# Attention with decay and a gated projection on one core: a fixed table of the order of work in place of a list scheduler

## The chip, the cores and the metric

The program runs on one core of a Trainium2 chip. The metric is the time on the device, in microseconds (us), from one launch; the kernel before took 556.66 us, the median of 3 runs (556.4 to 556.75). The core has five engines that follow their own instruction streams and wait for each other through semaphores: TensorE (PE in the profile, with its weight loads as PEld), VectorE (DVE), ScalarE (ACT), GpSimd (POOL), and SyncE (SP), which here issues the DMA transfers.

## The reference, cut to what matters

Eight batches of eight heads, 576 positions, head size 64. The output of the attention, with the heads side by side (512 columns), goes through a short causal convolution that makes a gate, a projection, the product, and a second projection.

```python
scores = scale * np.matmul(q, k.transpose(0, 1, 3, 2))
decay = cum[:, :, :, None] - cum[:, :, None, :]          # cum: running sum of log f
scores = np.where(causal, -1e9, scores + decay)
attn = np.exp(scores - np.max(scores, axis=-1, keepdims=True))
attn = attn / (np.sum(attn, axis=-1, keepdims=True) + 1e-09)
x = np.matmul(attn, v)                                    # per batch: 576 x 512
gate_pre = sum(conv_w[k] * xp[:, k:k + S, :] for k in range(5))
out = (sigmoid(gate_pre) * (x @ w_val)) @ w_out
```

## The kernel before, in words

The 64 heads are worked off as 32 pairs, four pairs to a batch. For a pair `i` the functions at L485 to L712 list its pieces of work:

- `load_pair`, `load_rest`: DMAs for q and k (`Xr`), v (`vt`) and, per head, a broadcast row of the decay (`dm`, `dl`); GpSimd masks the diagonal blocks (`sel`, L414).
- `plan_t` (from pair 4 on): `Xr` is split into a rounded part `Xh` (`TH`) and the rest `Xl` (`TL`, L494), so that three fast products replace a slow one.
- `plan_s`: scores on PE in three groups, `S` with u = 0 (blocks of 512 and 256 columns), u = 1 (384 and 128) and u = 2 (the last 64 rows, two banks). On each block DVE adds the decay and takes the row extreme (`red`, L562), ACT takes the exponential and its sum (`SX`, L566), DVE the reciprocal (`rec`), and `norm` scales the block (L375 on DVE and POOL, L373 on ACT).
- `plan_pt`: PE transposes the normalised blocks (`PT`, L607, L625, L626) into a bank, and ACT or DVE copies the bank out to `pt` (`PE`, L368).
- `plan_pv`: PE multiplies with v (`PV`, two halves), the result is copied out (`X`), split (`xh`, `xl`), and DVE makes five convolution taps (`conv`, L709; the first tap may stand on another engine, L375 or L373). For pairs 0 and 1 PE makes the taps (`CV`).
- `plan_moe`, per batch: the first projection (`Mv`, two pieces of six matmuls to a bank), the gating (`H`), a split (`hh`, `hl`, L755), the second projection (`Mo`), the copy out (`O`) and the store (`OD`).

Ahead of this stand the decay table, and the two weight matrices, decoded and split on DVE, ACT and POOL (`wv`, `wo`), in the first part of the run. Six groups of transposes of the identity (`warm`, L468) occupy PE while the first inputs are on their way.

A piece is a node of `Plan`: the engines that may run it with a cost for each, a function that emits its instructions, and what it reads and writes. `Plan.order` (L186) is a list scheduler: it keeps a clock per engine in a model, and takes again and again the piece that can start first, ties and near ties by a priority with tabled offsets (`OFF`, `PEN`, L47 to L88). In doing so it picks the engine of a piece that may run on several, and the PSUM banks that it takes (`seize`, `room`). Here is the choice itself:

```python
p, n, ts, t = min((p, n, ts, t) for ts, p, n, t in cand if ts <= t0 + SLACK[e])
if best is None or (ts, p) < best[:2]:
    best = (ts, p, n, e, t)
```

The instructions of each engine, and all DMAs together, are then bound to this order (L856 to L862), so an engine whose next instruction waits holds back all behind it. All eight PSUM banks are in use; a piece that takes a bank waits until its last user is done.

Of the kernel before, what the change touches and what calls it, by code (L numbers as in the profile page):

```python
# [37 lines left out]
BEGIN = {"PE": 0.7, "ACT": 2.0, "DVE": 0.7, "POOL": 0.6, "SP": 0.6, "DQ": 0.0}  # L38
LAG = {"PE": 0.17, "ACT": 0.2, "DVE": 0.17, "POOL": 0.25, "SP": 0.65, "DQ": 2.0, "bank": 0.15}
SAME = {"PE": 0.0, "ACT": 0.06, "DVE": 0.1, "POOL": 0.1, "SP": 0.0, "DQ": 0.0}  # L40
SLACK = {"PE": 0.0, "ACT": 0.0, "DVE": 0.0, "POOL": 0.0, "SP": 0.1, "DQ": 0.2}
SWITCH = 0.105
STICK = 319.71
PAIR = 0.002
PORT = {"rec", "TH", "TL", "norm", "conv", "hh", "hl", "xl", "xh", "sel", "wv", "wo", "cw", "start", "st0", "cut0", "cuth", "cutl"}
TICK, BUSY = 10.24 / 3, 3150.0
OFF = {  # L47
# [8 lines left out]
    "dec": (-55.39, -189.04, -128.16, 116.43, -6.04, -106.51), "diag": (-62.58, -70.54, 0.0, 0.0, 0.0, 0.0),  # L56
# [28 lines left out]
}  # L85
NONE = (0.0,) * 6


def phase(base):
# [5 lines left out]

# [808 lines left out]
```

## Time and profile before

| what | value |
|---|---|
| time, median of 3 runs | 556.66 us |
| the profiled execution: its span, first to last instruction | 555.8 us |
| PE busy | 524.2 us, 4412 matmuls |
| DVE busy | 455.7 us |
| ACT busy | 418.7 us |
| POOL busy | 280.2 us |
| mean granted clock of PE, as a share of full speed | 0.984 |

The time of the profiled execution by itself is its span; the median is 0.86 us above it. A busy share is a union over an engine's instructions, so a busy PE can still be in a pace slower than its best: the ends of matmuls are modelled. In lists of waits each row names the engine that waited, what it waited for, the total, the number and the longest. PEclk is the clock that PE was granted, 1.00 being 2.4 GHz and 0.50 being 1.2 GHz.

### The profile page before, as it was taken

The numbers are of one execution on the slowest core, as the hardware profiler recorded it, in microseconds if no ns is written. First come the engines' busy times: TensorE is split into PE (matmuls) and PEld (weight loads), VectorE is DVE, ScalarE is ACT, GpSimd is POOL, SyncE is SP. The second block draws the span as 40 slices with busy tenths as digits, with TensorE's granted clock in tenths as the row PEclk, the third lists the DMA queues.
The fourth block names the chain that finished last, engine by engine and source line by source line (L and its number), as shares of the span: only waits on it lengthen the run. The fifth ranks groups of instructions, "written<-read, shape, count | busy, mean of one in ns | idle before, by whom it ended". The sixth has DMA issues, their size and how long they took to land. (4 is left out here: it accounts for less than half of the span.)

```text
span 555.8 us, 12834 instructions
## 1 busy us (share of the span) xinstructions
PE 524.2 (94%) x4412; PEld 455.5 (82%) x4412; DVE 455.7 (82%) x1273; ACT 418.7 (75%) x1136; POOL 280.2 (50%) x377
## 2 busy tenths in 40 slices
PE   6687977999999999999999999999999999999997
PEld 5465765888889888898889978879888898989895
DVE  2987998988899988999788999889898887675560
ACT  2989888988867668678887978888998886673411
POOL 4223455576634823467456463645754688641200
PEclk8989897999999999999999999999999999999999
DMA  8867673545635575554565536855556544310102
GB/s 268 265 198 219 215 249 121 185 162 205 214 122 162 186 223 177 204 178 165 174 195 176 189 133 205 284 175 202 179 204 209 200 142 157 110 44 2 49 28 96
DMA packets 29905, 95.44 MB, mean 172 GB/s; under 512 B 3920, under 2 KB 3920, under 8 KB 29840
## 3 DMA queue, kind: packets, MB, share of 16 engines
q1 hardware_dynamic: 29696, 94.00, 51.1%
q8 instruction: 35, 0.57, 0.4%
q10 hardware_dynamic: 144, 0.62, 0.3%
q14 instruction: 30, 0.25, 0.2%
HBM read 84.69 MB, written 9.91 MB: 170 GB/s over the span
## 5 line engine op out<-in xcount | busy, mean ns | idle before, releaser
L566 ACT ACTIVATE P<-banks,negm 128x512 f32<-128x512 f32 (+3 forms) x256 | 132.0, 527 | 30.3 <-DVE negm L562 27.9
L562 DVE CUSTOM_DVE_ANT_0 banks<-banks,dm 128x512 f32<-128x512 f32 (+3 forms) x256 | 118.5, 517 | 20.2 <-PE banks L353 9.8
L709 DVE SCALAR_TENSOR_TENSOR gate<-x,cw,gate 128x576 f32<-128x576 f32 x120 | 106.3, 886 | 11.2 <-POOL gate L375 10.1
L353 PE MATMUL banks<-xh,wall 128*128 128x288 f32 x512 | 109.3, 299 | 0.6 <-DVE pt L368 0.3
L607 PE MATMUL banks<-ident,P 128*128 128x128 f32 x640 | 92.6, 283 | 15.2 <-ACT P L373 6.1
L353 PE MATMUL banks<-pt,vt 128*64 128x128 f32 (+2 forms) x1408 | 98.0, 293 | 0.2 <-ACT P L566 0.2
L607 PEld LDWEIGHTS banks<-ident,P 128*128 128x128 f32 x640 | 72.4, 142 | 29.6 <-ACT P L373 10.9
L353 PEld LDWEIGHTS banks<-pt,vt 128*64 128x64 f32 x1408 | 86.1, 138 | 11.9 <-issue 2.4
L414 POOL TENSOR_SCALAR_AFFINE_SELECT dm<-dm 128x256 f32<-128x256 f32 x126 | 60.1, 502 | 67.0 <-DMA dm<-decd 65.2
L353 PE MATMUL banks<-wall,hh 128*128 128x512 f32 x288 | 92.7, 403 | 0.4 <-ACT ot L782 0.4
L368 ACT COPY pt<-banks 128x512 f32<-128x512 f32 (+2 forms) x210 | 80.4, 448 | 11.3 <-PE banks L607 9.7
L353 PEld LDWEIGHTS banks<-xh,wall 128*128 128x128 f32 x512 | 83.7, 188 | 2.8 <-ACT P L566 0.9
L353 PE MATMUL banks<-xl,wall 128*128 128x288 f32 x256 | 75.4, 295 | 0.0
L373 ACT ACTIVATE P<-P,rz 128x256 f32<-128x256 f32 (+3 forms) x129 | 66.9, 571 | 3.4 <-DVE rz L576 3.2
L494 POOL TENSOR_TENSOR Xl<-Xr,Xh 128x640 fp32r<-128x640 f32 (+1 forms) x40 | 61.8, 1548 | 7.8 <-ACT Xh L368 6.1
L353 PE MATMUL banks<-Xh 128*128 128x288 f32 (+4 forms) x280 | 58.4, 343 | 3.6 <-DVE pt L368 1.6
L353 PEld LDWEIGHTS banks<-wall,hh 128*128 128x128 f32 x288 | 50.8, 188 | 9.7 <-ACT ot L782 0.7
L353 PE MATMUL banks<-wall,hl 128*128 128x512 f32 x144 | 56.5, 393 | 0.0
L368 DVE COPY pt<-banks 128x256 f32<-128x256 f32 (+2 forms) x110 | 46.0, 450 | 12.8 <-PE banks L607 6.2
L353 PE MATMUL banks<-Xh,Xl 128*128 128x288 f32 (+4 forms) x280 | 53.1, 313 | 0.0
L353 PE MATMUL banks<-Xl,Xh 128*128 128x288 f32 (+4 forms) x280 | 52.9, 313 | 0.0
L566 ACT ACTIVATION_READ_ACCUMULATOR P<-banks,negm 128x1 f32 x256 | 52.1, 204 | 0.0
(108 smaller groups left out, 873.7 us busy)
## 6 DMA issues: line engine op xcount, KB each, us to landing
dm<-decd SPq DMA_DIRECT2D x62, 640.0 KB, 5.2
Xr<-in_x_dram SPq DMA_DIRECT2D x31, 608.0 KB, 4.3
vt<-in_v_dram SPq DMA_DIRECT2D x32, 320.0 KB, 5.2
out_dram<-ot SPq DMA_DIRECT2D x36, 256.0 KB, 2.5
dl<-decd SPq DMA_DIRECT2D x62, 144.0 KB, 4.4
wu<-in_w_val_dram SPq DMA_DIRECT2D x2, 512.0 KB, 4.9
ot<-in_w_val_dram SPq DMA_DIRECT2D x2, 512.0 KB, 5.5
ot<-in_w_out_dram SPq DMA_DIRECT2D x2, 512.0 KB, 4.6
```

The source lines that it names most:

```text
L353: nc.tensor.matmul(out, lhsT=lhsT, rhs=rhs, start=start, stop=stop)
L368: (eng.copy if eng is nc.scalar else eng.tensor_copy)(out=out, in_=in_)
L373: eng.activation(out=out, in_=in_, func=AF.Copy, scale=col)
L414: nc.gpsimd.affine_select(out=t, in_=t, pattern=[[0, 2], [-1, P]], base=0, channel_multiplier=1, compare_op=ALU.is_ge, fill=-BIG)
L494: eng.tensor_tensor(out=Xl[r][:, a:e], in0=Xr[r][:, a:e], in1=Xh[r][:, a:e].bitcast(F32), op=ALU.subtract)
L562: nc.vector.tensor_tensor_reduce(out=sl, in0=sl, in1=add[:, o:o + ext], op0=ALU.add, op1=ALU.min, scale=-0.125, scalar=3.0e38, accum_out=n ...
L566: nc.scalar.activation(out=dst[:, o:o + ext], in_=bank(key)[:, c0:c0 + ext], func=AF.Exp, bias=negm[r][:, col], scale=-1.0, accum_out=zs[r ...
L607: nc.tensor.transpose(out=bank(key)[:, c:c + P], in_=Pt[m][:, BOFF[b] + P * j:BOFF[b] + P * j + P], identity=ident)
L709: eng.scalar_tensor_tensor(out=gt, in0=src, scalar=wt_, in1=gt, op0=ALU.mult, op1=ALU.add)
```

## The change

`Plan.order` no longer decides anything. A string of digits in base 64 (`TABLE`) holds, for each of the 2868 pieces that issue something, its number, its engine, and the banks that it takes; `order` reads it from front to back, and the functions are called in that order. The clocks, priorities, penalties and bank lists of the scheduler are gone, and with them a rule by which a piece that took a bank had to wait, in the list, for whatever the bank's later users depend on (`loose`). Some costs in the calls are other numbers (`S`, `PV`, `PT`, `SD`, `TH`, `rec`, `cut0`); nothing reads them any more. The pieces, their instructions and the buffers are the same.

```diff
@@ class Plan
-    def order(self, begin):
...
-            for e in ready:
-                cand = []
-                for n in ready[e]:
-                    nd = nodes[n]
-                    t = max(clock[e], at[n][e])
...
-            _, _, n, e, t = best
-            nd = nodes[n]
-            for x in nd["engs"]:
-                ready[x].remove(n)
-            for k in sorted(nd["take"], key=lambda k: -self.width[k]):
-                self.home[k] = self.seize(self.width[k], t)
...
-            self.trace.append((t, end, e, n))
+    def order(self, table):
+
+        at, done = 0, {nd["ends"]: n for n, nd in enumerate(self.nodes) if nd["ends"] is not None}
+        seen = set()
+        while at < len(table):
+            n, e = DIGITS.index(table[at]) * 64 + DIGITS.index(table[at + 1]), ENGINES[int(table[at + 2])]
+            nd = self.nodes[n]
+            at += 3
+            assert nd["deps"] <= seen and e in nd["engs"]
+            for k in nd["take"]:
+                self.home[k] = range(int(table[at]), int(table[at]) + self.width[k])
+                at += 1
+            seen.update((n, done.get(n, n)))
             yield nd["fn"], e
+        assert len(seen) == len(self.nodes)
...
-        for k in touch:
-            t = self.taker[k]
-            if t != n and k not in self.loose:
-                self.nodes[t]["deps"].update(d for d in deps if d < t)
...
-            pe("PV", (1.36, 1.47)[half], p, go, [*vk, *(("pt", m, n) for m in ms for n in names), *(("pt0", m) for m in ms)], [key],
+            pe("PV", (1.36, 1.515)[half], p, go, [*vk, *(("pt", m, n) for m in ms for n in names), *(("pt0", m) for m in ms)], [key],
...
-    for fn, e in plan.order(BEGIN):
-        if fn is not None:
-            fn(e)
+    for fn, e in plan.order("".join(TABLE.split())):
+        fn(e)
```

The table's first line of digits, for its form:

```
0240630040B30930C40E10b20430u000r010N40s000a20c20d10520F20H20I10G20z30e20J20f23k40q010h10K20g20740Y40L20k10l12940i20j20M20P10m42b30Q20S20T10R20U20V20v
```

The order of the pieces is another on every engine. Three places follow. In the rows below, line numbers of the changed kernel are about a hundred lower, since it is shorter: L507 there is L607 before, L253 is L353, L275 is L375, L314 is L414. A trailing `x4` counts equal instructions in a row.

**PE, the first transposes.** This is PE's stream in the kernel before, from the first transposes of pair 0 (`P0`, `P1` are its heads, `Pl0` its last rows) over scores of pair 1 (`Xr1`) to the second part of pair 0's transposes.

```order
L607 MATMUL banks_125<-ident_64,P0_79 128x128 x4
L607 MATMUL banks_125<-ident_64,P1_80 128x128 x4
L607 MATMUL banks_125<-ident_64,P0_79 128x128 x2
L607 MATMUL banks_125<-ident_64,P1_80 128x128 x2
L353 MATMUL banks_125<-Xr1_74 128x512 x2
L353 MATMUL banks_125<-Xr1_74 128x256 x2
L353 MATMUL banks_125<-Xr1_74 128x288 x2
L607 MATMUL banks_125<-ident_64,P0_79 128x128 x4
L607 MATMUL banks_125<-ident_64,P1_80 128x128 x4
L625 MATMUL banks_125<-ident_64,Pl0_82 128x128 x4
L626 MATMUL banks_125<-ident_64,Pl0_82 64x128
```

And the same place in the changed kernel:

```order
L368 MATMUL banks_125<-ident_64 128x128 x4
L507 MATMUL banks_125<-ident_64,P1_80 128x128 x2
L507 MATMUL banks_125<-ident_64,P0_79 128x128 x4
L507 MATMUL banks_125<-ident_64,P1_80 128x128 x4
L507 MATMUL banks_125<-ident_64,P0_79 128x128 x2
L253 MATMUL banks_125<-Xr1_74 128x384 x2
L253 MATMUL banks_125<-Xr1_74 128x128 x2
L253 MATMUL banks_125<-Xr1_74 128x512 x2
L253 MATMUL banks_125<-Xr1_74 128x256 x2
L253 MATMUL banks_125<-Xr1_74 128x288 x2
L507 MATMUL banks_125<-ident_64,P0_79 128x128 x4
L507 MATMUL banks_125<-ident_64,P1_80 128x128 x4
```

One of the six groups on the identity now stands in front of the first transposes, the blocks are transposed in another order, and the scores of pair 1 with 384 and 128 columns, which stood behind pair 0's transposes, stand in front of the second part of them.

**PE, the fifth pair.** In the kernel before, this follows the first half of pair 3's product with v: the scores of pair 4 with 512 and 256 columns (`Xh0`, `Xl0`), then at once the first transposes of pair 4 (`P2`), then the other half of pair 3's product (`pt0`, `vt1`).

```order
L353 MATMUL banks_125<-Xh0_75 128x512 x2
L353 MATMUL banks_125<-Xh0_75,Xl0_77 128x512 x2
L353 MATMUL banks_125<-Xl0_77,Xh0_75 128x512 x2
L353 MATMUL banks_125<-Xh0_75 128x256 x2
L353 MATMUL banks_125<-Xh0_75,Xl0_77 128x256 x2
L353 MATMUL banks_125<-Xl0_77,Xh0_75 128x256 x2
L607 MATMUL banks_125<-ident_64,P2_81 128x128 x4
L353 MATMUL banks_125<-pt0_84,vt1_88 64x192
```

In the changed kernel those scores stand further up, between transposes of pair 3, and the next transposes of pair 4 come behind these rows, a half of the product with v (12 rows like `banks_125<-pt0_84,vt1_88 64x128`), and five transposes of `Pl0`:

```order
L253 MATMUL banks_125<-xh0_97,wall_122 128x288
L253 MATMUL banks_125<-xl0_103,wall_122 128x288
L253 MATMUL banks_125<-xh0_97,wall_122 128x288
L253 MATMUL banks_125<-xh1_98,wall_122 128x288
L253 MATMUL banks_125<-xl1_104,wall_122 128x288
L253 MATMUL banks_125<-xh1_98,wall_122 128x288
L253 MATMUL banks_125<-Xh1_76 128x384 x2
L253 MATMUL banks_125<-Xh1_76,Xl1_78 128x384 x2
L253 MATMUL banks_125<-Xl1_78,Xh1_76 128x384 x2
L253 MATMUL banks_125<-Xh1_76 128x128 x2
L253 MATMUL banks_125<-Xh1_76,Xl1_78 128x128 x2
L253 MATMUL banks_125<-Xl1_78,Xh1_76 128x128 x2
```

A first half of a projection of batch 0, which needs only pairs 0 and 1 (`xh0`, `xl0`, `xh1`, `xl1`), and the scores of pair 5 (`Xh1`) with 384 and 128 columns have moved in front of pair 4's transposes. On the whole, counted over all pairs, PE changes between transposes or projections, scores, and products with v 131 times instead of 144.

**POOL, the first 30 us.** GpSimd's stream in the kernel before, from where the setup ends; `u32` and `h32` are the convolution's diagonal weights, `dm` and `dl` decay rows, `wall` the decoded weights, and `P<-P,rz` a normalisation.

```order
L690 TENSOR_TENSOR u32_111<-ident_64,cw_66 128x512
L375 TENSOR_SCALAR h32_112<-ident_64,cw_66 128x128
L441 MEMSET dm1_69 128x1280
L414 AFFINE_SELECT dm1_69<-dm1_69 128x2x128 x2
L442 MEMSET dl0_71 128x576
L417 TENSOR_TENSOR dl0_71<-dl0_71,tri_65 128x64
L414 AFFINE_SELECT dm2_70<-dm2_70 128x2x128 x2
L414 AFFINE_SELECT dm0_68<-dm0_68 128x2x128 x2
L417 TENSOR_TENSOR dl1_72<-dl1_72,tri_65 128x64
L375 TENSOR_SCALAR P0_79<-P0_79,rz0_93 128x128
L414 AFFINE_SELECT dm1_69<-dm1_69 128x2x128 x2
L417 TENSOR_TENSOR dl0_71<-dl0_71,tri_65 128x64
```

The same stretch in the changed kernel:

```order
L374 MEMSET tri_65 128x64
L376 AFFINE_SELECT tri_65<-tri_65 64x64 x2
L317 TENSOR_TENSOR dl0_71<-dl0_71,tri_65 128x64
L275 TENSOR_SCALAR P0_79<-P0_79,rz0_93 128x512
L275 TENSOR_SCALAR P1_80<-P1_80,rz0_93 128x512
L314 AFFINE_SELECT dm2_70<-dm2_70 128x2x128 x2
L275 TENSOR_SCALAR P0_79<-P0_79,rz0_93 128x384
L380 MEMSET x320_95 128x4
L314 AFFINE_SELECT dm0_68<-dm0_68 128x2x128 x2
L275 TENSOR_SCALAR Pl0_82<-Pl0_82,rz0_93 128x576
L590 TENSOR_TENSOR u32_111<-ident_64,cw_66 128x512
L275 TENSOR_SCALAR h32_112<-ident_64,cw_66 128x128
```

The clearing of `dm1` and `dl0` has gone to DVE, and four normalisations of pair 0 stand here where one stood, with the diagonal weights behind them.

Over the whole run the pieces that may run on more than one engine are shared out as follows:

| piece | DVE before, now | ACT before, now | POOL before, now |
|---|---|---|---|
| `norm` | 91, 75 | 143, 137 | 54, 76 |
| `PE` (copies of transposes) | 110, 103 | 210, 217 | |
| `X` (copies of the product with v) | 45, 18 | 19, 46 | |
| `conv` (the first tap) | 4, 2 | 2, 17 | 24, 11 |
| `TH` | 0, 14 | 25, 24 | 31, 18 |
| `TL` | 16, 29 | | 40, 27 |
| `hl` | 13, 21 | | 19, 11 |
| `xh` | 2, 9 | 30, 23 | |
| `xl` | 17, 14 | | 15, 18 |
| `O` | 8, 13 | 28, 23 | |
| `hh` | 6, 10 | 26, 22 | |
| `sel` (the small addition) | 2, 12 | | 30, 20 |

The load of the first pair's q and k, on ACT's queue before, is SP's sixth issue now.

## Rows read from the trace of the kernel before

**Rows 1.** The page: busy time of each engine with its share of the span, and the granted clock in 40 equal slices, in tenths.

```profile
PE 524.2 (94%) x4412; PEld 455.5 (82%) x4412; DVE 455.7 (82%) x1273; ACT 418.7 (75%) x1136; POOL 280.2 (50%) x377
...
PEclk8989897999999999999999999999999999999999
```

**Rows 2.** Busy time of each engine in stretches of the run (us from the span's start; number of instructions in brackets), then granted clock, DMA share and GB/s.

```profile
0.00:9.60 9.60, 5.05 (x26) 4.84 (x26) 3.60 (x12) 3.04 (x6) 2.96 (x19) 0.99 0.82 281
9.60:120.00 110.40, 92.63 (x698) 72.04 (x698) 96.44 (x275) 93.88 (x248) 52.77 (x70) 0.92 0.64 209
60.00:80.00 20.00, 18.33 (x142) 14.10 (x142) 18.49 (x44) 17.59 (x44) 11.76 (x15) 0.99 0.70 240
120.00:540.00 420.00, 414.49 (x3638) 368.95 (x3639) 355.56 (x988) 318.77 (x879) 224.44 (x289) 1.00 0.49 163
540.00:555.80 15.80, 12.04 (x54) 9.63 (x52) 0.10 (x1) 2.99 (x5) 0.00 (x0) 0.99 0.23 84
```

**Rows 3.** What PE waited for from 0 to 120 us: total us, times, longest us. There are twelve such rows, 21.9 us in all.

```profile
PE banks L607 <- ACT P L373: 5.8, 7, 2.0
PE banks L353 <- DVE gate L821: 3.1, 1, 3.1
PE banks L607 <- ACT P L566: 2.6, 1, 2.6
PE banks L607 <- POOL P L375: 2.0, 1, 2.0
...
PE banks L468 <- POOL ebias L431: 1.4, 1, 1.4
PE banks L353 <- DVE pt L368: 1.1, 2, 0.9
...
PE banks L625 <- ACT Pl L373: 0.2, 1, 0.2
```

**Rows 4.** The same from 120 us to the end: nine rows, 5.0 us in all; the first, the second, and the last.

```profile
PE banks L607 <- DVE x L368: 1.7, 2, 1.4
PE banks L353 <- DVE pt L368: 0.8, 2, 0.5
...
PE banks L353 <- ACT P L566: 0.2, 1, 0.2
```

**Rows 5.** The sum over the three stretches between 12.8 and 540 us in which the granted clock is 0.50: 29.86 to 33.27, 57.16 to 60.58 and 84.47 to 91.30 us. Columns as in rows 2.

```profile
sum 13.66, PE 12.37 PEld 9.14 DVE 11.65 ACT 11.55 POOL 4.26; mean PE 4.12 PEld 3.05 DVE 3.88 ACT 3.85 POOL 1.42
```

**Rows 6.** PE's timeline: start, duration, instruction and count, and in brackets the idle time before it with what ended it.

```profile
25.17 1.24 PE L353 MATMUL banks<-Xr 128*128 128x288 f32 x4 [1.41 <-ACT Pl L566]
28.99 1.19 PE L607 MATMUL banks<-ident,P 128*128 128x128 f32 x8 [2.58 <-ACT P L566]
...
55.82 0.63 PE L607 MATMUL banks<-ident,P 128*128 128x128 f32 x4 [1.95 <-POOL P L375]
```

**Rows 7.** PE's timeline from 78 to 86 us, in the same form.

```profile
78.21 0.29 PE L353 MATMUL banks<-Xl,Xh 128*128 128x288 f32 x1
78.43 0.45 PE L353 MATMUL banks<-Xh 64*128 64x384 f32 x2
...
79.45 1.75 PE L353 MATMUL banks<-pt,vt 128*64 128x128 f32 x24
81.54 0.50 PE L353 MATMUL banks<-Xh 64*128 64x512 f32 x2 [0.34 <-ACT Pl L566]
...
83.79 0.39 PE L353 MATMUL banks<-Xh 64*128 64x256 f32 x2 [1.29 <-ACT P L566]
...
85.57 1.27 PE L607 MATMUL banks<-ident,P 128*128 128x128 f32 x4 [1.15 <-ACT P L373]
```

**Rows 8.** The chain that ended last, in order of time: start, duration, engine, line and count.

```profile
405.24 0.44 PE banks L607 x4
...
419.56 0.80 PE banks L353 x6
```

**Rows 9.** Groups of instructions over the whole run: count, busy us and mean ns of one, then the engine's idle time before them.

```profile
L494 POOL TENSOR_TENSOR Xl<-Xr,Xh 128x640 fp32r<-128x640 f32 (+1 forms) x40 | 61.8, 1548 | 7.8 <-ACT Xh L368 6.1
...
L375 POOL TENSOR_SCALAR P<-P,rz 128x512 f32<-128x512 f32 (+3 forms) x48 | 32.8, 694 | 35.2 <-DVE rz L576 25.4 <-ACT wall L368 2.8 <-ACT gate L798 2.4
...
L368 DVE COPY x<-banks 128x192 f32<-128x192 f32 (+1 forms) x45 | 19.6, 447 | 8.1 <-PE banks L353 7.9
...
L494 DVE TENSOR_TENSOR Xl<-Xr,Xh 128x576 fp32r<-128x576 f32 (+1 forms) x16 | 14.1, 895 | 0.0
...
L368 ACT COPY x<-banks 128x384 f32<-128x384 f32 (+1 forms) x19 | 7.6, 405 | 11.1 <-PE banks L353 10.9
```

**Rows 10.** The timeline of all engines at the start: the load of the first pair, and PE's first weights from it.

```profile
0.83 0.38 ACTq L380 DMA_DIRECT2D Xr<-in_x_dram  x1
...
11.85 0.80 PEld L353 LDWEIGHTS banks<-Xr 64*128 64x128 f32 x4
```

**Rows 11.** The convolution taps on DVE from 440 to 480 us.

```profile
L709 DVE SCALAR_TENSOR_TENSOR gate<-x,cw,gate 128x576 f32<-128x576 f32 x12 | 10.3, 854 | 0.1
```

**Rows 12.** The same taps from 500 to 540 us.

```profile
L709 DVE SCALAR_TENSOR_TENSOR gate<-x,cw,gate 128x576 f32<-128x576 f32 x12 | 12.5, 1043 | 8.3 <-POOL gate L375 8.0
```

**Rows 13.** The engines in these two stretches, columns as in rows 2.

```profile
440.00:480.00 40.00, 40.00 (x344) 36.08 (x342) 32.38 (x96) 29.10 (x86) 33.95 (x46) 1.00 0.37 127
500.00:540.00 40.00, 40.00 (x308) 36.72 (x307) 24.45 (x44) 11.73 (x26) 5.45 (x7) 1.00 0.07 27
```

More of the change, by code (lines that the diff above doesn't have):

```diff
@@ L37 @@
 MS = 0.2222
[L38 to L45, printed above, removed]
@@ L86 @@
-NONE = (0.0,) * 6
-def phase(base):
-    return sum(base >= x for x in (0.95, 3, 6, 11, 28))
+ENGINES = ("PE", "ACT", "DVE", "POOL", "SP")
+DIGITS = "0123456789abcdefghijklmnopqrstuvwxyzABCDEFGHIJKLMNOPQRSTUVWXYZ-_"
+TABLE = """
+0240630040B30930C40E10b20430u000r010N40s000a20c20d10520F20H20I10G20z30e20J20f23k40q010h10K20g20740Y40L20k10l12940i20j20M20P10m42b30Q20S20T10R20U20V20v
+002d001232e02l20W10y32j22o0452m12h23a40X30o40_22x062f20A32k12i12r22t20w30-
+12c32g12s10t001122n23c42B31212E11742Q002p22q12v22w13e44n42K012u12y24t43g44r42z12C32D23i41021323m32M022N12O032P22R21422L12A24l41512G12I11621i43z0453p02
@@ L94, with __init__ @@
+03LL3LR2LO2LS2LT2M40LZ2LW2L-2L_2Md01M22M52M62M72M800M90GB2Ma1GC4Me0Mf1Mb4Mi00Mj0Mk1Mg4Ml4Mn01Ms00Mo0Mp1Mt0Mq4Mu1Mv4
+"""
 class Plan:
-    def __init__(self, banks):
+    def __init__(self):
         self.nodes = []
-        self.free = {n: 0.0 for n in range(banks)}
         self.home = {}
@@ L113, in __init__, with bank @@
         self.width = {}
-        self.users = {}
-        self.taker = {}
-        self.loose = set()
-    def bank(self, key, width=1, loose=False):
+        self.taken = set()
+    def bank(self, key, width=1):
         self.width[key] = width
-        if loose:
-            self.loose.add(key)
         return key
@@ L136, in add @@
             self.readers[k] = []
-        take, touch = [], []
-        for k in (*writes, *reads):
-            if k in self.width and k not in touch:
-                touch.append(k)
-                self.users.setdefault(k, []).append(n)
-                if k not in self.taker:
-                    self.taker[k] = n
-                    take.append(k)
-        deps.discard(n)
-        self.nodes.append(dict(cls=cls, engs=engs, base=float(prio), phase=phase(prio), prio=prio * PAIR + OFF.get(cls, NONE)[phase(prio)], fn=fn, deps=deps, take=take, touch=touch,
-                               cols=cols, mode=mode, ends=ends))
-        for k in touch:
-            t = self.taker[k]
-            if t != n and k not in self.loose:
-                self.nodes[t]["deps"].update(d for d in deps if d < t)
+        touch = list(dict.fromkeys(k for k in (*writes, *reads) if k in self.width))
+        take = [k for k in touch if k not in self.taken]
+        self.taken.update(take)
+        deps.discard(n)
+        self.nodes.append(dict(cls=cls, engs=engs, base=float(prio), fn=fn, deps=deps, take=take, touch=touch, cols=cols, mode=mode, ends=ends))
         return n
@@ L160, in dma @@
         return m
-    def seize(self, width, t):
-        fit = [n for n in self.free if all(self.free.get(n + k, 1e18) <= t + 1e-9 for k in range(width))]
-        n = min(fit) if width == 1 else max(fit)
-        for k in range(width):
-            del self.free[n + k]
-        return [n + k for k in range(width)]
-    def room(self, widths):
-        for t in sorted(set(self.free.values())):
-            at = sorted(n for n in self.free if self.free[n] <= t)
-            left = list(at)
-            for w in sorted(widths, reverse=True):
-                fit = [n for n in left if all(n + k in left for k in range(w))]
-                if not fit:
-                    break
-                n = min(fit) if w == 1 else max(fit)
-                for k in range(w):
-                    left.remove(n + k)
-            else:
-                return t
-        return None
@@ L514, in plan_s @@
                 name = ("S", i, h, u, j if u == 0 else 0)
-                keys[n] = new(name, 2 if u == 2 else 1, loose=i == 0)
+                keys[n] = new(name, 2 if u == 2 else 1)
             pairs = ((0, 1), (2, 3))
@@ L724, in plan_moe @@
             for half, (lo, hi) in enumerate(((0, 288), (288, 576))):
-                key = new(("Mv", b, jj, half), loose=b == B - 1 and jj < 2)
+                key = new(("Mv", b, jj, half))
                 p = m0 + MS * (2 * jj + half)
```

180 lines of the change are left out of this document (76 added, 104 removed), and 17 rows, old and new, of tables (OFF, PEN).

## The prediction

> **What bounds the kernel now.** I read the page first [rows 1]: PE is busy 94% of the span, DVE 82%, ACT 75%, POOL 50%. The reader is to see that the granted clock is below full in the first fifth of the slices alone. Then the engines by stretch [rows 2]: from 120 to 540 us PE is busy 414.5 of 420 us, while from 9.6 to 120 us it is busy 92.6 of 110.4 us and DVE and ACT 96.4 and 93.9. So there are two regimes: a long one in which PE sets the pace and the others run beside it, and a first one in which PE, DVE and ACT take turns in waiting. Then PE's waits [rows 3, 4]: 21.9 us of the listed ones lie before 120 us, 5.0 us after it. Of the early ones 4.5 us belong to the start (1.4 and 3.1, for the identity and the decay table); 17.4 us are waits for normalised blocks, for banks and for copies. Then the clock: three stretches of 0.50 [rows 5] hold 13.66 us, with PE busy in 12.37 of them. At full speed that work would take half, so up to 6.2 us are lost there. The two waits from 25 to 29 us [rows 6] come just ahead of the first of these, the wait of 1.95 ahead of 55.82 just before the second, the three near 82 to 86 us [rows 7] around the third.
>
> The Trainium skill says on its front page ("Trainium Kernel Development and Optimization", "Performance Expectations") that matmul busy time is a poor measure of how near a kernel is to its limit. Here the trace agrees: the stretches at half clock count as 12.37 us busy [rows 5]. By the page's rule the 94% is no floor; by the row alone the gain could not pass the span less the busy time, 31.6 us. The sum below stays far under that.
>
> **The change part by part.** No instruction is added or removed, so nothing is paid for in kind. The pace of the tail is fixed: from 540 us on PE runs only the last projection [rows 2], which needs everything before it; I cost it at nothing. What the order does I take in five terms.
>
> *1. Waits from 9.6 to 120 us.* At pair 4, in the kernel before, PE has from the end of the 384 and 128 column scores (79.45) to the first transposes only a half of a product with v (1.75) and one scores group (79.45 - 78.43 = 1.02) to do, 2.8 us; the blocks were ready 6.1 us after the scores, at 85.57, and 0.34 + 1.29 + 1.15 us of waiting stand between [rows 7]. In the new order I count behind the same scores 15 transposes at 0.11 (0.44 for four), half a projection at 0.80 [rows 8], two scores groups at 1.02 and two halves of products at 1.75 [rows 7]: 1.65 + 0.80 + 2.04 + 3.5 = 8.0 us, more than 6.1. These waits should go. At pair 0 the scores of pair 1 that moved up cover about 1 us of the 3.99 us waited there [rows 6], and four normalisations stand on POOL where one stood, which spares ACT. Over the whole program I counted, at the fastest tenth of each kind's start-to-start times in the trace, the PE work between a scores group and each of its 224 transposing pieces: it is under 5 us for 20 of them before and for 3 now, under 8 us for 70 before and for 23 now.
>
> How much of it becomes time is set by what else is full. The work that DVE and ACT have to do up to the same point of PE's stream is about the same (pieces counted along both orders, with the trace's durations, give 1% more on DVE and 2% more on ACT by the time PE has done 80 us of work at its best pace). DVE is busy 96.4 of 110.4 us there. The fullest stretch that the rows show is 18.49 of 20 us, 92.5% [rows 2]. At that share 96.4 us of work take 104.3 us: 6.1 us less than now. The waits and the clock together offer 17.4 + 6.2 = 23.6 us, so DVE is what limits it. The bounds are 0 (the waits move, DVE's share stays at 87%) and 14 us (DVE without a gap); I take 6.1, by the row. At the very start nothing is expected: PE waits there for the decay table, which hangs on the load of f. The two clearings that go to DVE lie in its idle time (3.60 of 9.60 us busy [rows 2]); if that cover were gone they would delay the table by their length.
>
> *2. Waits after 120 us.* Of 5.0 us [rows 4] I take off 3, about the share by which short distances to the scores become rarer (70 to 23); bounds 0 and 5.
>
> *3. Turns of PE between kinds of work*, 144 to 131. At 78.21 the last full-width matmul is followed by scores 0.22 us later, where six such matmuls take 0.80, 0.13 each [rows 7, 8]: 0.09 a turn, 13 x 0.09 = 1.2 us less. Bounds: nothing, and twice as much.
>
> *4. Copies of transposes.* Of the 64 halves of products with v, 17 have under 4 us of PE work between their last transposes and themselves before, 32 now. PE waited for such a copy four times, 1.9 us in all, at most 0.9 [rows 3, 4]. Over the 17 close ones that is 0.11 each, so 15 more cost 1.7 us. Bounds: nothing, and 15 x 0.9 = 13.5 us, each as late as the worst.
>
> *5. Work that changes engine.* DVE gets 13 of the subtractions `TL` at 0.895, but gives 27 copies `X` at 0.447 away to ACT, where one takes 0.405 [rows 9]; with all lines of the table of the change I make it some 11 us more on DVE, 11 more on ACT and 40 less on POOL. From 120 us on DVE is busy 85% and ACT 76% [rows 2]; 11 us more in 420 is under 3 points each, so PE's work hides it: cost 0. The bound above is all 11 us, if DVE were on the path throughout; below, 0. The load of the first pair's q and k moves from ACT's queue to behind five issues on SP. PE took its first weights from it at 11.85, 11 us after the issue [rows 10], so a few microseconds of delay are hidden; past that each would delay the first scores.
>
> The Trainium skill speaks against the mix in "SBUF — State Buffer", section "Who interferes with whom": a DVE instruction with two SBUF inputs and a GpSimd instruction that reads SBUF exclude each other. The taps are of that kind, and the trace has them at 854 ns where POOL is busy 33.95 of 40 us, and at 1043 ns where it is busy 5.45 [rows 11 to 13]: the trace does not show POOL slowing them. By the rows the term is 0; by the rule see the last rival.
>
> Sum against the execution's own time: 555.8 - 6.1 - 3.0 - 1.2 + 1.7 = 547.2; the median of the runs stood 0.86 above that span, so 548.1 us.
>
> **Rivals.** *More goes than DVE's fullest stretch suggests.* If DVE runs without a gap up to 120 us: -14, -5, -1.2 and no cost in copies: 535.6 + 0.9 = 536.5. For it: POOL is busy 52.8 of 110.4 us, so more of DVE's share could be taken over. Against: DVE gets more work, not less.
>
> *The waits only move.* DVE's share stays at 87% up to 120 us and the late waits come back as waits for banks: -1.2 + 1.7, so 557.2. For it: at 81.54 and 83.79 PE waited for banks, not for blocks [rows 7], and the new order holds more scores in the same eight banks at once. Against: the counted distances.
>
> *Copies late (slower).* The halves of products with v stand nearer to their transposes, and the copies between them sit in the queues of DVE and ACT, each with 11 us more to do. At 0.9 us for each of 15 [term 4]: 555.8 - 6.1 - 3.0 - 1.2 + 13.5 = 559.0, 559.9 as a median. It decides from about 0.7 us each, where 15 of them eat the 10.3 us of gains. Against: in the trace these waits are short.
>
> *DVE and POOL in each other's way (slower).* 22 more normalisations on POOL at 0.694 [rows 9] are 15.3 us; if each held a DVE instruction back for its length and DVE were on the path: 548.1 + 15.3 = 563.4. This is the rule of the SBUF page, against which [rows 11 to 13] stand, and POOL has 40 us less to do in all.
>
> **How the numbers follow.** Forecast 0.63, with its own range of 541 to 554 us (early waits from 0 to 12 us); more goes, 0.09; waits only move, 0.10; copies late, 0.12; DVE against POOL, 0.04; between the forecast's range and no change, 0.02. What a measurement can tell from no change is 0.2%, 1.1 us, so 555.5 to 557.8 counts as the same. Faster is 0.63 + 0.09 + 0.02 = 0.74, same 0.10, slower 0.16. The likeliest case gives 548.1. A range of 540 to 559 leaves out most of the first rival below and the worse half of the slower ones above, some 0.18 together.
>
> **What would show it.** Term 1 is right if from 9.6 to 120 us the listed waits of PE fall well below 17 us, the stretches of half clock near 30, 57 and 85 us get fewer or shorter, and DVE's share rises over 90%; the stretch around pair 4's transposes should show no wait of a microsecond. It is wrong if PE's waits there carry other names (banks, `X`) with the same total. Term 4 is wrong if PE's waits for `pt` exceed 5 us. Term 5 is wrong if DVE's share from 120 us on rises over 92% and PE's busy share there falls. The forecast fails as a whole if PE, from 120 us on, is idle more than 10 us.

## The result, and the profile after

The changed kernel takes 540.42 us, the median of 4 runs (539.51 to 541.72), against 556.7 us for the kernel before on the same chip: a ratio of 0.9702, 95% interval 0.9666 to 0.9738, 16.3 us less. The forecast was 548.1 us. The time lies in the range of 540 to 559, but at its lower edge, and 0.6 us outside the range that the likeliest case had for itself (541 to 554). The profiled execution has a span of 539.0 us, 16.8 less than before.

The page of the kernel after, the lines of [rows 1]:

```profile
PE 515.9 (96%) x4412; PEld 448.6 (83%) x4412; DVE 468.1 (87%) x1288; ACT 424.5 (79%) x1160; POOL 241.9 (45%) x338
...
PEclk9999999999999999999999999999999999999999
```

The same 4412 matmuls count as 8.3 us less of busy PE, and no slice has a clock below nine tenths. The stretches of [rows 2], after:

```profile
0.00:9.60 9.60, 6.17 (x28) 5.01 (x28) 6.26 (x18) 4.43 (x8) 2.98 (x16) 1.00 0.70 231
9.60:120.00 110.40, 99.95 (x829) 79.63 (x829) 101.55 (x307) 103.96 (x287) 54.60 (x78) 1.00 0.72 234
60.00:80.00 20.00, 19.18 (x190) 16.00 (x188) 19.83 (x57) 19.65 (x55) 9.07 (x11) 1.00 0.85 287
120.00:540.00 420.00, 409.77 (x3559) 363.95 (x3555) 360.34 (x966) 316.12 (x866) 184.32 (x245) 1.00 0.48 160
```

From 9.6 to 120 us PE starts 829 matmuls where it started 698, and DVE and ACT are busy 92% and 94% of the time, where they were 87% and 85%. The last row is no loss: it holds the end of the run, which now comes at 539.

PE's waits up to 120 us, to be read beside [rows 3]; there are 14 rows, 13.3 us in all:

```profile
PE banks L253 <- DVE pt L268: 3.7, 4, 2.6
PE banks L368 <- POOL ident L323: 3.0, 1, 3.0
PE banks L525 <- ACT pt L268: 1.5, 2, 1.3
PE banks L507 <- ACT P L273: 0.9, 1, 0.9
...
PE banks L253 <- DVE gate L358: 0.4, 1, 0.4
...
PE banks L253 <- ACT pt L268: 0.2, 1, 0.2
```

Here L507 and L525 are transposes, L368 the transposes of the identity at the start, L253 all other matmuls (scores, products with v, projections), L273 ACT's normalisation, L268 the copies out of PSUM. The waits for normalised blocks, 5.8 and 2.0 us in the first and fourth of [rows 3], are down to 0.9 and a few tenths; what is left at the head of the list are copies (`pt`). From 120 us on, beside [rows 4], there are eight rows and 5.1 us, so the total is what it was:

```profile
PE banks L253 <- ACT P L466: 2.1, 4, 0.8
...
PE banks L507 <- ACT P L273: 0.2, 1, 0.2
```

The drop of the listed waits, 26.9 to 18.4 us, is 8.5 us; PE's busy time falls by 8.3. Together they are the whole 16.8 us.

**Where in the run it comes.** The two streams of PE are ordered differently, so I compared them by work done: each group of matmuls counted at the fastest tenth of its kind's start-to-start times in the trace of before. PE has done 40 us of such work at 67.9 us before and at 61.5 after (6.4 earlier), 60 us of it at 101.3 and 85.0 (16.3 earlier), 80 us at 124.9 and 109.1 (15.8), 200 us 14.5 earlier, 320 us 19.1 earlier, the end 16.8 earlier. All of the gain is there after 85 us, and the rest of the run neither adds nor takes. The stretches of before, from the start to the marks of 20, 40 and 60 us of work, and then from 9.6 us to the mark of 80:

```profile
0.00:39.60 39.60, 29.08 (x168) 21.64 (x169) 28.16 (x86) 26.31 (x67) 14.05 (x37) 0.91 0.75 245
39.60:67.90 28.30, 23.84 (x162) 18.57 (x160) 24.25 (x73) 24.68 (x65) 11.76 (x17) 0.94 0.71 217
67.90:101.30 33.40, 27.01 (x236) 20.73 (x235) 30.38 (x79) 28.37 (x76) 19.00 (x22) 0.90 0.54 181
...
9.60:124.90 115.30, 97.23 (x742) 76.02 (x742) 100.04 (x286) 97.69 (x257) 56.83 (x75) 0.93 0.63 203
```

The same of the kernel after:

```profile
0.00:35.20 35.20, 26.85 (x169) 19.24 (x170) 28.22 (x91) 25.79 (x69) 13.75 (x37) 1.00 0.87 271
35.20:61.50 26.30, 23.33 (x159) 16.44 (x159) 23.48 (x74) 26.08 (x72) 11.37 (x17) 1.00 0.68 230
61.50:85.00 23.50, 21.91 (x218) 18.52 (x217) 23.36 (x71) 23.32 (x67) 12.63 (x14) 1.00 0.72 244
...
9.60:109.10 99.50, 89.34 (x750) 70.20 (x748) 91.49 (x278) 93.52 (x256) 48.11 (x69) 1.00 0.73 239
```

The third row is the main one. For the same work of PE (236 matmuls before, 218 after, of other sizes) the time falls from 33.40 to 23.50 us, and DVE's part from 30.38 to 23.36: it is busy 99% of this stretch, and so is ACT. The last rows say the same of the longer stretch: DVE's share is 92.0% now, 86.8% before, and its work between 9.6 us and the same point of PE's work is 8.5 us less. Of these, 2.7 us have only moved: they are done before 9.6 us, where DVE is busy 6.26 us instead of 3.60. From the start of the run to the mark DVE does 97.75 us instead of 103.64, 5.9 less. Up to the mark it has made 19 copies of transposes where it had made 35 (7.6 us less), ACT has made 14 more of them and 14 fewer normalisations, and POOL 7 more normalisations.

**The fifth pair.** PE's timeline after, at the place of [rows 7]:

```profile
69.84 0.27 PE L253 MATMUL banks<-Xl,Xh 64*128 64x128 f32 x2
70.05 1.09 PE L507 MATMUL banks<-ident,P 128*128 128x128 f32 x8
...
73.14 1.64 PE L253 MATMUL banks<-pt,vt 128*64 128x192 f32 x20 [0.38 <-DVE pt L268]
74.71 0.40 PE L253 MATMUL banks<-xh,wall 128*128 128x288 f32 x1
...
76.70 1.53 PE L253 MATMUL banks<-pt,vt 128*64 128x128 f32 x24
78.16 0.66 PE L525 MATMUL banks<-ident,Pl 128*128 128x128 f32 x4
...
78.76 1.72 PE L507 MATMUL banks<-ident,P 128*128 128x128 f32 x12
```

Between the last of pair 4's 384 and 128 column scores (69.84) and its transposes (78.76) stand transposes of pair 3, scores, two halves of products and the half projection at 74.71, 8.9 us in all, of which one wait of 0.38 us, where [rows 7] show 0.34, 1.29 and 1.15.

### The profile page after: what moved, and what is told of

Its sections match the earlier page's. It is cut to its first block, busy times and chain, and to the rows that moved or that the text cites. A ratio compares the mean times of both kernels' runs of the same rounds, so it can differ in the third digit from the quotient of the medians.

```text
span 539.0 us, 12792 instructions
## 1 busy us (share of the span) xinstructions
PE 515.9 (96%) x4412; PEld 448.6 (83%) x4412; DVE 468.1 (87%) x1288; ACT 424.5 (79%) x1160; POOL 241.9 (45%) x338
## 4 chain that ended last, share of the span: by engine, by line
PE 61%; DVE 19%; ACT 8%; DMA 5%; issue 4%; SPq 1%; POOL 0%; DVEq 0%; ACTq 0%; POOLq 0%
PE banks L253 51%; PE banks L507 8%; DVE banks L462 5%; DVE gate L609 4%; DMA dl<-decd 3%; ACT P L466 3%; PE banks L525 2%; DVE pt L268 1%; DMA out_dram<-ot 1%; ACT pt L268 1%; SPq L280 1%; DVE P L275 1%; DVE Xl L394 1%; DMA Xr<-in_x_dram 1%; DVE negm L462 1%
## 5 line engine op out<-in xcount | busy, mean ns | idle before, releaser
L466 ACT ACTIVATE P<-banks,negm 128x384 f32<-128x384 f32 (+3 forms) x256 | 135.3, 544 | 25.6 <-DVE negm L462 22.4
L253 PE MATMUL banks<-xh,wall 128*128 128x288 f32 x512 | 119.0, 305 | 1.5 <-ACT P L466 0.7
L609 DVE SCALAR_TENSOR_TENSOR gate<-x,cw,gate 128x576 f32<-128x576 f32 x120 | 109.0, 913 | 1.2
L268 ACT COPY pt<-banks 128x256 f32<-128x256 f32 (+2 forms) x217 | 90.3, 451 | 21.7 <-PE banks L507 14.6
L253 PE MATMUL banks<-pt,vt 128*64 128x128 f32 (+2 forms) x1408 | 95.7, 290 | 3.9 <-DVE pt L268 3.0
L314 POOL TENSOR_SCALAR_AFFINE_SELECT dm<-dm 128x256 f32<-128x256 f32 x126 | 62.3, 520 | 80.6 <-DMA dm<-decd 57.6
L507 PE MATMUL banks<-ident,P 128*128 128x128 f32 x640 | 93.1, 276 | 4.9 <-ACT P L466 1.7
L253 PEld LDWEIGHTS banks<-pt,vt 128*64 128x64 f32 x1408 | 83.9, 137 | 15.1 <-issue 5.7
L253 PE MATMUL banks<-wall,hh 128*128 128x512 f32 x288 | 93.3, 405 | 1.2 <-ACT P L466 1.2
L253 PEld LDWEIGHTS banks<-xh,wall 128*128 128x128 f32 x512 | 86.1, 188 | 4.8 <-ACT P L466 1.4
L507 PEld LDWEIGHTS banks<-ident,P 128*128 128x128 f32 x640 | 72.8, 140 | 17.1 <-ACT pt L268 2.7
L275 POOL TENSOR_SCALAR P<-P,rz 128x512 f32<-128x512 f32 (+3 forms) x67 | 48.2, 725 | 72.8 <-DVE rz L476 45.1
L253 PE MATMUL banks<-xl,wall 128*128 128x288 f32 x256 | 75.4, 295 | 0.0
L273 ACT ACTIVATE P<-P,rz 128x512 f32<-128x512 f32 (+3 forms) x117 | 65.6, 586 | 3.8 <-DVE rz L476 3.4
L253 PEld LDWEIGHTS banks<-wall,hh 128*128 128x128 f32 x288 | 50.2, 188 | 10.3 <-ACT P L466 1.7
L253 PE MATMUL banks<-Xh 128*128 128x288 f32 (+4 forms) x280 | 57.2, 338 | 1.3 <-DVE h L641 0.6
L253 PE MATMUL banks<-wall,hl 128*128 128x512 f32 x144 | 56.6, 393 | 0.0
L466 ACT ACTIVATION_READ_ACCUMULATOR P<-banks,negm 128x1 f32 x256 | 55.9, 218 | 0.0
L253 PE MATMUL banks<-Xl,Xh 128*128 128x288 f32 (+4 forms) x280 | 53.1, 313 | 0.1
L253 PE MATMUL banks<-Xh,Xl 128*128 128x288 f32 (+4 forms) x280 | 53.1, 313 | 0.0
L253 PEld LDWEIGHTS banks<-xl,wall 128*128 128x128 f32 x256 | 48.2, 188 | 0.2
```

The lines of the kernel that those rows point to most:

```text
L253: nc.tensor.matmul(out, lhsT=lhsT, rhs=rhs, start=start, stop=stop)
L268: (eng.copy if eng is nc.scalar else eng.tensor_copy)(out=out, in_=in_)
L273: eng.activation(out=out, in_=in_, func=AF.Copy, scale=col)
L275: eng.tensor_scalar(out=out, in0=in_, scalar1=col, scalar2=0.0, op0=ALU.mult, op1=ALU.add)
L314: nc.gpsimd.affine_select(out=t, in_=t, pattern=[[0, 2], [-1, P]], base=0, channel_multiplier=1, compare_op=ALU.is_ge, fill=-BIG)
L466: nc.scalar.activation(out=dst[:, o:o + ext], in_=bank(key)[:, c0:c0 + ext], func=AF.Exp, bias=negm[r][:, col], scale=-1.0, accum_out=zs[r ...
```

## The experiments

In the mixes below, "40 us" and "60 us" are the marks of PE's work described above. Where the trace of a mix is compared with that of before, the marks are counted in the same way and read between two groups of matmuls; for the new kernel that gives 6.4, 15.7 and 16.6 us at 40, 60 and 80. Where a mix puts a piece at a place at which its bank is still taken, it has the bank that has been free longest. All orders are written out as a table, as in the changed kernel. In times against the kernel before, each set of runs has its own runs of that kernel on the same chip (medians 557.2 to 557.7 us).

**Which part of the run brings it.** The tables of five kernels, as a sketch:

```diff
-table = new
+table = new[:60us] + rest(old)               # new head
+table = old[:60us] + rest(new)               # new tail
+table = new[:320us] + rest(old)              # mix at 320
+table = new[:40us] + rest(old)               # new to 40
+table = old[:40us] + rest(new[:60us]) + rest(old)   # new from 40 to 60
```

> The changed kernel's table up to the point where PE has done 60 us of its work at its best pace, then the order, engines and (where free) banks of the kernel before. Theory A (the gain is made in the first 85 us alone): 541, within 538 to 544. Rival B (the gain is spread over the run by shorter waits and fewer turns; the first eighth of PE's work brings an eighth of it): 554.5, over 550.

> The reverse: the kernel before up to the same point of PE's work, then the changed kernel's table. Theory A: 556, within 553 to 559. Rival B: 542.5, under 547. If A and B are both part of it, the two runs' gains add up to 16 us.

New head: 543.58 us, ratio 0.9747 (0.9716 to 0.9777). New tail: 561.09 us, ratio 1.0057 (1.0030 to 1.0084). The head alone carries 14 of the 16.6 us that the ratio of the full change stands for. The tail brings nothing. Counted by the marks, the trace of the new head is 18.3 us ahead of the kernel before at 60 us of work and 12.4 at 80, so it loses 5.9 us just behind its joint; that of the new tail (the slowest of its ten runs) is 2.2 us behind at 60 and 5.5 at 120.

> The changed kernel's table until PE has done 320 us of its work, then the order and engines of the kernel before. In the two traces the changed kernel is 19.1 us ahead at that point and 16.8 at the end. If the later part of the old order is better by itself: 538, under 539.5. If a joint costs what it costs in the other mixes (2 to 4 us): 541 to 543.

542.53 us, ratio 0.9708 (0.9675 to 0.9740). The mark of 320 us, where the new kernel was 19.1 us ahead, is no place from which the old order does better: this mix and the new kernel can't be told apart.

> The new table until PE has done 40 us of its work at its best pace, then what is left in the order, engines and banks of before. The two traces stand 6.4 us apart at that mark and 16.3 us apart at 60. Theory A (each stretch of the new order brings its own part, nothing later depends on it): 6.4 us less than before, less the 2 to 4 us that joints cost in the other mixes: 550 to 554 us. Theory B (the new beginning leaves work on DVE and ACT in such a state that the later stretch runs well in any order): the mix comes near the new kernel, 540 to 545. Theory C (what is gained up to 40 us is only lent, by work on DVE and ACT that is put off): 556 or more.

> The order of before until PE has done 40 us of its work, then the pieces that the new table has up to 60 us and that are not yet done, in its order, with its engines and banks, then before again. Two joints. Theory A (local): 9.9 us less than before, and 2 to 4 us for each joint: 551 to 553 us. Theory B (the middle stretch needs the new beginning): no gain, 556 or more. A time under 549 would say that the stretch by itself carries all of what it shows.

New to 40: 548.36 us, ratio 0.9828 (0.9800 to 0.9857), 9.6 us. The trace of this run is 8.8 us ahead of the kernel before at the mark of 40, 9.6 at that of 60, and 10.9 at the end. It gains while it follows the new table, and the old order behind it adds next to nothing; that is theory A, only with a joint that costs nothing visible, so the time lies below A's 550. That 9.6 us are more than the 6.4 us of the new kernel's own trace at this mark speaks for no later effect: the new head and the mix at 320, which have the same table up to there, are 9.1 and 8.8 us ahead at 40.

New from 40 to 60: 558.53 us, ratio 1.0016 (0.9989 to 1.0043), no gain as a whole, as theory B had it. Its marks show another reason than B's. Its trace is 0.4 us behind the kernel before at 40 us of work, 3.5 behind at 50, 2.5 ahead at 60 and 2.3 behind at 80. So from 50 to 60 it gains 6.0 us, where the new kernel gains 7.4, and it loses 3.1 us behind its first joint and 4.8 behind the second, as the new head did behind its own. Whether the stretch needs the new beginning can't be told from this run: the joints take what it gains.

**Order or engines.** The order of one kernel with the engines of the other, over the whole run; banks as above:

```diff
-for piece, engine in new: emit(piece, engine)
+for piece, _ in new: emit(piece, engine_of[old][piece])   # new order, old engines
+for piece, _ in old: emit(piece, engine_of[new][piece])   # old order, new engines
```

> The changed kernel's order of all pieces and its banks, but each piece that may run on several engines on the engine that the kernel before gave it. If the order does it (theory A): under 546. If the new shares of the engines do it (rival C): over 552. A value over 557 says that order and engines only work together.

> The order and banks of the kernel before, with the engines of the changed kernel. Theory A: over 553. Rival C: under 546. A value well over 557 says that order and engines only work together.

623.85 us, ratio 1.1186 (1.1154 to 1.1219), and 612.0 us, ratio 1.0979 (1.0938 to 1.1020). Neither half of the change is an improvement; each by itself is 10 to 12% slower than the kernel before. The loss is in the long stretch, where PE had hardly waited: at the mark of 80 the two traces are 0.6 and 1.8 us behind the kernel before, at the end 64.6 and 53.7. The longest row of PE's waits from 120 us on, of the new order with old engines (22 rows, 51.3 us in all):

```profile
PE banks L242 <- ACT pt L257: 10.6, 11, 2.4
```

And of the old order with new engines (23 rows, 40.3 us):

```profile
PE banks L496 <- ACT x L257: 9.5, 7, 3.7
```

PE waits for copies up to 3.7 us at a time. That these copies come late because others stand ahead of them in their engine's queue is how I read it; the two rows are only the longest of many. (In the kernels with tables of their own, line numbers are 11 lower than in the changed kernel: L242 there is L253, L496 is L507.)

**Two kinds of pieces by themselves.** The new kernel, with the engines of before for one kind of piece in the part up to 60 us:

```diff
-emit(piece, engine_of[new][piece])
+emit(piece, engine_of[old if kind(piece) == "PE" and at < mark60 else new][piece])    # old copies
+emit(piece, engine_of[old if kind(piece) == "norm" and at < mark60 else new][piece])  # old norms
```

> The new kernel, but in the part up to 60 us of PE's work the copies of transposes stand on the engine that they had before: 17 go from ACT back to DVE, 7 from DVE to ACT. DVE gets 4.9 us more to do there (10 at 0.49), ACT 4.3 less. If DVE's amount of work sets the pace of the first part, the time rises by 4 to 5 us: 544 to 546. If it is set by which engine is free at the moment when a piece is due in this order, each misplaced copy waits or makes others wait: 24 of them at a few tenths of a microsecond, 546 to 552. If neither matters: 540 to 542.

> The new kernel, but in the part up to 60 us of PE's work the normalisations stand on the engine that they had before (20 of them differ). ACT gets 5.9 us more to do (10 at 0.59), DVE some 1.8 less, POOL 4.7 less. If DVE's amount of work sets the pace of the first part, the time falls by up to 2 us or stays: 538 to 541. If ACT's does: 545 to 547. If it is set by which engine is free when a piece is due: up by several microseconds though DVE has less to do, 545 to 552.

Old copies: 547.43 us, ratio 0.9823 (0.9792 to 0.9854), 6.7 us above the new kernel by the ratios. Old norms: 548.51 us, ratio 0.9833 (0.9806 to 0.9859), 7.3 us above. The stretch from 9.6 to 120 us with old copies:

```profile
9.60:120.00 110.40, 97.62 (x788) 76.88 (x785) 102.58 (x307) 96.26 (x268) 52.05 (x74) 0.98 0.67 222
```

And with old norms, with PE's first wait there:

```profile
9.60:120.00 110.40, 96.36 (x774) 74.24 (x772) 94.46 (x286) 102.76 (x280) 46.36 (x66) 0.97 0.68 218
```

```profile
PE banks L496 <- ACT P L262: 5.6, 6, 1.7
```

With old copies DVE is as full as in the new kernel (102.58 against 101.55 us) and ACT has room (96.26). With old norms it is the other way round: DVE has 16 us free and ACT is at 93%; PE waits 5.6 us for ACT's normalisations, as in [rows 3]. So DVE's amount of work alone does not set the pace: with old norms DVE has less to do than in the new kernel (some 1.8 us by the count before the run), and the time is 7.3 us longer. Either of the two engines can be the one that PE waits for, and the new table keeps both at 92 and 94%. That ACT's amount alone sets it was put at 545 to 547 for old norms, just under what was measured, but it falls with old copies, which lighten ACT and are slower too.

**Does DVE's work set the pace?** Both kernels without the decoding of the second weight matrix, some 11.6 us of DVE and 5.8 us of ACT in the first part:

```diff
+        def put(eng):
+            return lambda c, d, p_, fn, *a: eng(c, d, p_, fn if c != "wo" else lambda: None, *a)
...
-        dve(cls, one, p, lambda: nc.vector.tensor_scalar(
+        put(dve)(cls, one, p, lambda: nc.vector.tensor_scalar(
...
-        return y.bitcast(F32)
+        return zz if cls == "wo" else y.bitcast(F32)
```

> The changed kernel without the decoding of the second weight matrix (20 instructions on DVE, about 11.6 us, and 8 on ACT, about 5.8 us, all in the first 85 us; the rest of the computation reads other data in its place, so the output is not the reference's). If DVE's and ACT's work sets the pace of the first part (theory E1): 7 to 11 us less, 530 to 534. If PE's waits there are latencies of the chain scores, exponential, scaling, transposes (rival E2): at most 3 us less.

> The same work left out of the kernel before, its order otherwise unchanged. If DVE's work limited the first part there as the prediction had it (E1): 7 to 11 us less, 546 to 550. If PE waited there for latencies and the order of pieces, with DVE busy on work that nobody waited for (E2): at most 4 us less, 553 or more.

From the new kernel: 536.59 us, ratio 0.9610 (0.9576 to 0.9644), 3.8 us below the new kernel by the medians and 5.1 by the ratios. From the kernel before: 553.25 us, ratio 0.9900 (0.9866 to 0.9934), 4.5 us by the medians, 5.6 by the ratio. In both, less than half of what was taken off DVE comes back. The stretch from 9.6 to 120 us in the new kernel without the decoding:

```profile
9.60:120.00 110.40, 105.15 (x882) 84.82 (x879) 99.19 (x300) 103.46 (x290) 56.22 (x80) 0.98 0.73 239
```

PE is at 95%, ACT stays at 94% and DVE drops to 90%: what was freed on DVE soon meets ACT and PE. The expectations for this pair gave clear figures on either side, and the measured ones lie between, nearer to the smaller: DVE's work is part of the limit, not the whole of it.

**Is the clock a cause?** The kernel before with transposes of the identity in front of two of the transposing pieces, at the places where its clock falls:

```diff
-            def go(key=key, m=m, blocks=blocks):
+            def go(key=key, m=m, blocks=blocks, fill={(2, 0, (3,)): 14, (4, 0, (2, 0)): 8}.get((i, h, blocks), 0)):
                 c = 0
+                for _ in range(fill):
+                    nc.tensor.transpose(out=bank(key)[:, 0:P], in_=ident, identity=ident)
```

> The kernel before with 14 extra transposes of the identity ahead of pair 2's first transposes (where PE waited 1.95 us for a normalised block, ahead of the half-clock stretch from 57.16 us) and 8 ahead of pair 4's first (1.15 us, inside the stretch from 84.47); each group goes into the bank that the real transposes fill next, and is overwritten. Theory D1 (the fallen clock costs time of its own, and keeping PE occupied keeps it up): the stretch at 57 us is gone and the time falls by 1.5 to 4 us, to 553 to 555.5. Rival D2 (the clock is only a sign of the waits; PE waits for blocks either way): same within 0.5 us, or up to 1 us longer.

559.28 us, ratio 1.0025 (0.9997 to 1.0053). PE's timeline at the two places, the filler (L606) and the transposes behind it (L609):

```profile
56.25 1.75 PE L606 MATMUL banks<-ident 128*128 128x128 f32 x14 [1.87 <-ACT P L566]
57.84 1.36 PE L609 MATMUL banks<-ident,P 128*128 128x128 f32 x11
...
83.72 1.09 PE L606 MATMUL banks<-ident 128*128 128x128 f32 x8
84.97 0.55 PE L609 MATMUL banks<-ident,P 128*128 128x128 f32 x3
```

The stretches at half clock from 57.16 and from 84.47 us, 10.2 of the 13.66 us of [rows 5], are gone, and no time is gained. The filler at 56.25 still waited 1.87 us, for an exponential on ACT, and then held the real transposes up by 1.6 us; that at 83.72 took 1.25. So the clock was not to be had for nothing: 2.8 us of filler stand against the faster PE.

How much faster PE became, this profile can't say by itself. In it the first half-clock stretch, at the start of the run and far ahead of the filler, is 6.8 us long where it was 3.4 before. The stretch from 9.38 to 16.20 us, before and with the filler:

```profile
9.38:16.20 6.82, 6.62 (x34) 4.38 (x35) 3.08 (x15) 2.90 (x7) 4.12 (x7) 0.75 0.84 242
...
9.38:16.20 6.82, 6.56 (x22) 3.95 (x24) 2.45 (x11) 2.27 (x6) 4.12 (x7) 0.54 0.84 243
```

So half-clock time falls by 6.8 us here, not by 10.2, and the mean clock rises from 0.984 to 0.990. All runs of the set together say the same: the mean clock is 0.982 in the 17 of the kernel before and 0.989 in the 12 with the filler, which makes 3.6 us less lost to half clock. By that count 0.8 us should be left after the filler, a ratio of 0.9986; the interval begins at 0.9997. The filler does not pay. What a half-clock stretch costs when nothing is put in its place, no run shows. That it costs something is likely: among the 17 runs of the kernel before, the time falls by 3.4 us per 0.01 of mean clock, and by 1.8 us in each of the two other sets of 13, where 0.01 of clock is 5.6 us of the span. But waits and lost clock come together there, so this is no proof.

## Why the prediction was right, and where it was off

The direction and the place were right, the size was half of it. That the time still lies in the stated range is luck: 0.4 us separate it from the lower end, and one of the four runs (539.51) lies below. The forecast's terms against an account of the two profiled spans:

| term | forecast, us | shown, us |
|---|---|---|
| 1, waits from 9.6 to 120 us, without products' waits for `pt` | -6.1 with the clock | -10.3 |
| 1, half clock, counted as the prediction did | in the above | up to -6.2 |
| 2, waits after 120 us, without those for `pt` | -3.0 | +0.6 |
| 3, turns of PE, with all else in its busy time | -1.2 | -2.1 |
| 4, products' waits for `pt` | +1.7 | +2.3 |
| 5, work that changes engine | 0 | not seen |
| the start (identity, decay table) | 0 | -1.1 |
| sum | -8.6 | -16.8 |

*Term 1, the step that failed.* The place was read rightly: the waits beyond the start fell from 17.4 to 9.9 us, no half-clock stretch is left in the first part, pair 4 has no wait of a microsecond. What was wrong is the cap. It rested on two figures: DVE's fullest share, 92.5%, and DVE's work up to the same point of PE's stream, "1% more". The first came out to within half a per cent, at 92.0%. The second did not: from 9.6 us to the mark of 80, DVE did 91.49 us instead of 100.04, 8.5% less. With the old amount at the share shown, 100.04 / 0.920 = 108.7 us, 6.6 less than 115.3, close to the forecast's 6.1; the rest, up to the 15.8 us of the mark, is the smaller amount. Of that, 2.7 us were moved into DVE's idle time ahead of 9.6 us, which the prediction noted for the two clearings but did not count, and 5.9 us are missing altogether. The whole-run table of pieces by engine, where DVE gains, hides this. The prediction does not show the count behind its 1%; along both lists, with the durations of the two traces, I find 3% less on DVE by the mark of 80, and 4 to 9% less at marks from 70 to 90. The 16 copies that DVE no longer makes there are the largest part. And as a mechanism the cap was too simple: taking 11.6 us off DVE brought 4 to 6 us, and giving DVE less and ACT more cost 7 (old norms). No one engine's amount bounded the first part before. That PE, DVE and ACT waited for each other in turn is the reading that the runs leave; they don't show it piece by piece.

*Term 2* brought nothing: the waits after 120 us are 5.1 us as before. The distances counted over the whole program are longer there too, but the marks stand still from 85 us on, and the new tail by itself is not faster. In that stretch PE is busy nearly all the time (404.5 of 410 us from 120 to 530; to the end of the run it is idle 9.3 us, just under the 10 that would have made the forecast fail, and it was 9.3 before too), and there was little to take. The step that failed here is to price waits by the distances: they got rarer, the waits did not.

*Term 3* can't be separated. The 2.1 us hold every change of pace in PE's busy time, and no run changed the turns alone.

*Term 4* was nearly right in size, +2.3 us by products with v. Its sign was set at 5 us of waits for `pt`; counting transposes that wait for the bank of such a copy too they are 6.5, and 2.63 of them are a single wait at 29.57 us, in pair 0, which in the mix at 320, with the same table there, is 0.57. By the letter the sign says wrong; by its price the term was short by 0.6 us. That each of 15 would cost 0.9, the rival of late copies, did not come.

*Term 5* held. DVE is busy 86% from 120 us on (360.34 of 420), under the 92 that would have spoken against it. The rule of the Trainium skill's page "SBUF — State Buffer" ("Who interferes with whom"), that a DVE instruction with two SBUF inputs and a GpSimd instruction that reads SBUF exclude each other, shows no price here: DVE's taps from 440 to 480 us take 831 ns with POOL busy 11.45 of 40 us, where [rows 11, 13] had 854 ns with 33.95.

*The rivals.* "The waits only move" and the two slower ones fell. "More goes" gave 536.5 and lies 3.9 us from the result, nearer than the forecast. Its condition, a DVE without a gap up to 120 us, was met only from 61.5 to 85 us; much of the gain came by less work on DVE up to the mark, where I had held more work against it.

What stays open: which pieces of the new order bring the 9 to 10 us between the marks of 40 and 60, and whether they would without the new beginning; the one run on that loses as much at its joints as it gains. The engines chosen for copies and for normalisations are each worth about 7 us in the new order, but these parts don't add up. The banks were never changed by themselves, and how much of PE's 8.3 us is clock no run separates.

## What to carry to other kernels

An order and a choice of engines are one decision: half of a better plan can be worse than the old one, so compare plans whole, or change them together over a stretch from the start. To bound what a new plan brings, count for every engine what it has to do along the new order up to several marks of the bounding stretch, from the start of the run, and not over the whole run. And by the same marks, look at where a mixed order gains and loses before its total time is taken for a verdict on the part that was exchanged. A half clock or a long wait points to the place; what its removal brings has to be measured.

## What was not expected of the hardware

Keeping PE's clock at full speed with idle transposes was possible at both places, with 14 and 8 of them, and their 2.8 us ate what it brought (1.0025). The same table gives another clock from run to run: in the 43 runs of the kernel before that the sets hold, its mean lies between 0.977 and 0.991, and the first half-clock stretch was 3.4 us long in its profile and 6.8 in that of the kernel with filler, which differs only later. And the same pieces in the same order took 623.85 instead of 540.42 us only because engines were exchanged for others that may run them as well: the instructions of each engine are bound to the listed order, and a piece on an engine for which that order was not made cost far more here than the difference between the engines, which for a copy of transposes (three shapes mixed) is 451 ns on ACT against 432 on DVE.

The last figures are from these groups of the kernel after (count, busy us and mean ns, then idle time before them):

```profile
L268 ACT COPY pt<-banks 128x256 f32<-128x256 f32 (+2 forms) x217 | 90.3, 451 | 21.7 <-PE banks L507 14.6 <-PE banks L525 2.8 <-DVE pt L268 2.6
...
L268 DVE COPY pt<-banks 128x256 f32<-128x256 f32 (+2 forms) x103 | 42.7, 432 | 4.7 <-PE banks L526 2.1 <-PE banks L507 1.1 <-ACT pt L268 1.0
```
